# Attention's 64-token halves on the two halves of the partitions, merged TensorE visits, and an earlier start of the first MLP

## The chip, the cores and the metric

One NeuronCore of a Trainium2 chip. The metric is the device time of one execution in microseconds, median of the runs given. Engine names in the profile: PE is TensorE, PEld its weight loads, DVE VectorE, ACT ScalarE, POOL GpSimd, SP SyncE (it issues the DMAs).

## The reference

4 sequences of 768 tokens, 8 heads of 32 columns. A gated linear attention runs over them in chunks with a carried 16 x 32 state per head; its output, [3072, 256], passes a gated MLP (RMS norm, 1536 hidden) and a second MLP (2048 hidden).

```python
y_intra = einsum('bhij,bhjd->bhid', CB * L, xc)            # L: decays inside the chunk, causal
y_inter = einsum('bhin,bhnd->bhid', Cc, state) * decay_to_i
state = decay_full * state + sum_j(Bc_j xc_j decay_from_j)
xn = x / sqrt(mean(x*x) + 1e-6) * rms_g                      # x: the attention's output
x = (silu(xn @ w_gate) * (xn @ w_val)) @ w_out
out = ((x @ w_in) * clip(x @ w_in + 3, 0, 6) / 6) @ w_out2
```

The weights arrive as 64-bit floats.

## The kernel before, in words

**Tiling.** The attention is cut into 24 chunks of 128 tokens (4 sequences, 6 positions); each chunk is two halves of 64 tokens. Four chunks, one of each sequence, make a block of 512 tokens. The first MLP (stage A) runs over 6 blocks x 12 steps of 128 hidden columns, the second (stage B) over 6 blocks x 16 steps. Each matrix product is done as three fp32r products of high and low parts (`mm3`, L640 to L643): a group of six matmuls of 512 columns. A step of stage A (`step`, L647) has three groups: two `hidden` (gate and value, into `hps`) and one `result` (into `acc`); a step of stage B has one of each two kinds. Between them ScalarE applies Silu or Relu (`gate`, L668), VectorE multiplies (`prod`, L676), ScalarE makes the high part (`hi`, L684) and GpSimd or VectorE the low part (`lo`, L688, recorded at L242).

**A chunk** (`attention`, L319) loads one packed tensor (`cb`, 1152 columns, in which the two heads of a pair are padded with zeros), the decays `L` and the prefix products `P`. For the first four chunks the decays are spread over the partitions by TensorE (`spread_a`, L354, tile `aps`), later ones come by DMA from a copy in DRAM (`azero`). VectorE runs the product scan (L367). TensorE is visited three times: `score` (L389) with `grow` (L407), `inner` (L450), and `mean` (L480, the sum of squares of each token). Each of these fp32 matmuls leaves two records in the trace.

**The norm of a block** (`norm`, L502): on [128, 4] scalars VectorE does the inverse root (for block 0 ScalarE's Sqrt and a reciprocal, later a guess by integer arithmetic and three Newton rounds, with `y` in PSUM), TensorE broadcasts the result (`back`, L531, tile `rps`), VectorE scales x (L537), and `split` (L560) makes high and low parts.

**PSUM.** Two banks for `acc` and three pairs of banks (`w`), which the chunks (two pairs each) and the MLP's steps (one pair each) take in turns.

**What sets the order.** `Plan` (L33) is a list scheduler: every operation is entered with engine costs in ns, with what it reads and writes, and with a boost. It goes through simulated time, takes on each engine the operation with the longest tail plus boost, and emits all in that order, so each engine's queue is fixed. Buffers taken in turns also fix the order of their first writers (L64). Attention of the next block carries a boost of 6000, that of the first block 15000 (L28, L29); weights (`weights`, L579: load, four conversions, high and low part) carry none. `AT` (L26) says behind which step of a block the next block's chunks and norm are entered. While TensorE has nothing in the plan's first part, `fill` (L156) puts in idle matmuls (`idle`, L303). The loop over all this is at L748 to L776.

## Time and profile before

| | us |
|---|---|
| median of 3 runs | 679.15 |
| lowest and highest run | 677.57, 680.35 |
| span of the profiled execution | 677.3 |

The profile is that of one execution, of which no other time than its span is listed. TensorE is busy 97% of the span, VectorE and ScalarE 44%, GpSimd 42%. Matmuls overlap, so a record of 0.39 us stands for about 0.23 us of TensorE's time when others follow; lengths are therefore read from start to start. In a row of stretches the first number is the length, then each engine's busy us with its count.

### The profile page before, as it was taken

To read this page: it belongs to the slowest core of one execution; us is meant where nothing else is said; L and a number is where in the kernel's file an instruction comes from. 1 tells how busy PE (TensorE), PEld (TensorE's weight loads), DVE (VectorE), ACT (ScalarE), POOL (GpSimd) and SP (SyncE) were. 2 spreads that over 40 slices of the span, in tenths; PEclk is the share of its full clock that TensorE was granted. 3 is DMA by queue.
4 is the path that set the end of the run, shared out by engine and by line. 5 is a ranking of instruction groups with operands and counts; after the bars stand their busy time and mean duration, and the time that the engine had idled before them with its cause. 6 is when DMAs were issued, how large, how long until landed. Compare 5 with 4: busy or idle time off the path is not lost.

```text
span 677.3 us, 10507 instructions
## 1 busy us (share of the span) xinstructions
PE 657.6 (97%) x4188; PEld 529.0 (78%) x4188; DVE 301.0 (44%) x507; ACT 298.2 (44%) x494; POOL 282.7 (42%) x239
## 2 busy tenths in 40 slices
PE   8978999999999999999999999999999999999997
PEld 7856777778778778877867777888888888888886
DVE  4799853352234334332578773232322322332222
ACT  1576632322333223313366654445454545445543
POOL 3354453333433332432232435455454545545443
PEclk9888999999999999999999999999999999999999
DMA  5995203210221123030023420000000000000000
GB/s 196 318 320 188 95 1 95 70 55 20 91 67 44 56 65 100 1 118 1 0 94 125 142 76 0 1 0 32 1 0 32 0 32 0 1 32 0 32 0 32
DMA packets 24465, 42.92 MB, mean 63 GB/s; under 512 B 2112, under 2 KB 15712, under 8 KB 24416
## 3 DMA queue, kind: packets, MB, share of 16 engines
q1 hardware_dynamic: 24416, 42.25, 19.2%
q8 instruction: 33, 0.54, 0.3%
q14 instruction: 16, 0.13, 0.1%
HBM read 38.90 MB, written 3.34 MB: 62 GB/s over the span
## 4 chain that ended last, share of the span: by engine, by line
PE 80%; DVE 10%; ACT 3%; issue 3%; DMA 2%; POOL 1%; SPq 0%; POOLq 0%; ACTq 0%; DVEq 0%
PE hps L643 41%; PE acc L643 30%; DVE cv L608 2%; PE sps L394 2%; PE sps L463 2%; DMA L<-azero 1%; DVE cv L603 1%; DVE p L679 1%; ACT p L671 1%; PE sps L457 1%; PE sps L482 1%; DVE yT L608 1%; POOL gl L242 1%; PE sps L412 1%; PE aps L359 1%
## 5 line engine op out<-in xcount | busy, mean ns | idle before, releaser
L242 POOL TENSOR_TENSOR gl<-p,gh 128x512 fp32r<-128x512 f32 x160 | 214.3, 1341 | 239.8 <-ACT gh L686 233.1
L686 ACT CAST gh<-p 128x512 fp32r<-128x512 f32 x168 | 104.5, 622 | 94.7 <-PE acc L643 92.0
L681 DVE SCALAR_TENSOR_TENSOR p<-p,hps 128x512 f32<-128x512 f32 x96 | 65.9, 687 | 170.1 <-ACT p L673 170.1
L643 PE MATMUL hps<-xh,w1h 128*128 128x512 f32 x288 | 96.3, 416 | 7.9 <-ACT p L671 4.8
L673 ACT ACTIVATE p<-hps,half 128x512 f32<-128x512 f32 x96 | 66.3, 691 | 83.8 <-POOL gl L242 82.9
L679 DVE TENSOR_TENSOR p<-p,hps 128x512 f32<-128x512 f32 x72 | 49.3, 685 | 97.7 <-PE hps L643 75.8
L643 PE MATMUL hps<-xh,w1l 128*128 128x512 f32 x288 | 90.2, 395 | 0.0
L643 PE MATMUL hps<-xl,w1h 128*128 128x512 f32 x288 | 89.9, 393 | 0.0
L643 PE MATMUL acc<-gh,w2h 128*128 128x512 f32 x192 | 74.7, 389 | 0.0
L643 PE MATMUL acc<-gh,w2l 128*128 128x512 f32 x192 | 74.7, 389 | 0.0
L643 PE MATMUL acc<-gl,w2h 128*128 128x512 f32 x192 | 74.7, 389 | 0.0
L671 ACT ACTIVATE p<-hps 128x512 f32<-128x512 f32 x72 | 43.0, 597 | 64.6 <-POOL gl L242 33.2
L643 PEld LDWEIGHTS hps<-xh,w1h 128*128 128x128 f32 x288 | 50.0, 190 | 24.6 <-ACT p L671 8.9
L643 PEld LDWEIGHTS hps<-xh,w1l 128*128 128x128 f32 x288 | 54.6, 189 | 12.4
L643 PEld LDWEIGHTS hps<-xl,w1h 128*128 128x128 f32 x288 | 54.6, 190 | 12.3
L643 PE MATMUL hps<-xh,w2h 128*128 128x512 f32 x192 | 59.6, 391 | 1.5 <-DVE p L679 0.8
L643 PE MATMUL hps<-xl,w2h 128*128 128x512 f32 x192 | 59.2, 389 | 0.0
L643 PE MATMUL hps<-xh,w2l 128*128 128x512 f32 x192 | 59.1, 389 | 0.0
L643 PE MATMUL acc<-gh,w1h 128*128 128x512 f32 x144 | 59.0, 410 | 0.0
L643 PE MATMUL acc<-gl,w1h 128*128 128x512 f32 x144 | 56.3, 391 | 0.0
L643 PE MATMUL acc<-gh,w1l 128*128 128x512 f32 x144 | 56.2, 390 | 0.0
L242 POOL TENSOR_TENSOR bh<-cb,L 128x256 f32<-128x256 f32 x24 | 17.1, 713 | 76.4 <-PE sps L412 48.3
(94 smaller groups left out, 814.3 us busy)
## 6 DMA issues: line engine op xcount, KB each, us to landing
cb<-comb SPq DMA_DIRECT2D x20, 576.0 KB, 8.1
raw<-w SPq DMA_DIRECT2D x16, 512.0 KB, 3.4
L<-azero SPq DMA_DIRECT2D x40, 128.0 KB, 3.3
yT<-w SPq DMA_DIRECT2D x6, 768.0 KB, 9.2
rawx<-w SPq DMA_DIRECT2D x6, 768.0 KB, 9.7
out<-yT SPq DMA_DIRECT2D x12, 256.0 KB, 2.0
P<-pref SPq DMA_DIRECT2D x24, 64.0 KB
cb<-comb SPq DMA_DIRECT2D x4, 320.0 KB, 4.0
```

What stands on the lines that cost most here:

```text
L242: eng[e].tensor_tensor(out=out, in0=a, in1=b, op=op)
L359: pe.matmul(out=ps[64 * q:64 * q + 64, p * CH:(p + 1) * CH], rhs=az[:, q], lhsT=eye[:96, c:c + 1].to_broadcast([96, SC]), start=True, stop ...
L394: pe.matmul(out=bank2(ws[p // 2], "sps")[:, p % 2, c * SC:(c + 1) * SC], lhsT=cb[r, BN + c * 128:BN + (c + 1) * 128], rhs=cb[r, CT + c * S ...
L412: pe.matmul(out=v()[32 * p:32 * p + 32, 1, 384 + 64 * c:448 + 64 * c], lhsT=b[:, h], rhs=cb[:, 64 * (4 * c + p):64 * (4 * c + p) + 64], st ...
L463: pe.matmul(out=o[p][c], lhsT=cb[:, q:q + 64], rhs=SM[:, p, SC * c:SC * c + SC], start=False, stop=True, skip_group_check=True)
L608: dve.scalar_tensor_tensor(out=u, in0=T[kr].bitcast(I32)[:, :, 1], scalar=-0x80000000, in1=u, op0=ALU.bitwise_and, op1=ALU.bitwise_or)
L643: pe.matmul(out=o, lhsT=a, rhs=c, start=first and i == 0, stop=last and i == len(seq) - 1)
L671: act.activation(out=p[:, :n], in_=T["w", hid][:, 0, :n], func=AF.Silu)
L673: act.activation(out=p[:, :n], in_=T["w", hid][:, 0, :n], func=AF.Relu, scale=1.0 / 6.0, bias=half)
L679: dve.tensor_tensor(out=p, in0=p, in1=h, op=ALU.mult)
L681: dve.scalar_tensor_tensor(out=p, in0=p, scalar=1.0, in1=h, op0=ALU.min, op1=ALU.mult)
L686: act.copy(out=t[:, :n], in_=T["p", i][:, :n])
```

## The change

- The two halves of a chunk lie on partitions 0 to 63 and 64 to 127. `cb` shrinks to 896 columns: C is padded now, x and B are not. Score has 8 matmuls of 32 rows, 64 weight columns and 128 moving columns (before: 128 and 64); grow 8 of 64 rows (before 128); inner 16 of 64 rows and 32 weight columns and 8 of 32 rows as before. VectorE masks the grown state (`mask`).
- A visit of TensorE does `score` and `grow` of chunk k and `inner` of chunk k - 1, with a drain inside `inner`. A block has four visits (the first block one more).
- The norm works on [128, 512]: high and low parts of the squares, four matmuls with a matrix of ones, then all further steps at full width in SBUF; for block 0 it is done chunk by chunk at 128 columns.
- The first four chunks load `L` from the input and clip it; `spread_a` goes.
- PSUM: in the start two pools of four banks for chunks; then two `acc` banks, two single `h` banks for the MLP, four for chunks; from step 9 of the last block but one on four `hb` banks in place of these.
- Weight tiles 0 and 1 carry boosts of 12000 and 10000. ScalarE reads the Silu table behind the last root of block 0.
- The idle matmuls only begin when the start's PSUM pool closes.

```diff
-AT = {0: 0, 2: 1, 4: 2, 6: 3, 8: 4}
+W0 = 12000
+AT = [1, 3, 5, 7]
+AT_NORM = 8
+NCB = 3
...
-            fn, ns, t, cold, until = self.fill
+            fn, ns, after, cold, until = self.fill
+            t = 1 + next(s for s, i, _, _ in out if i == after)
+            cold += t
...
-    ps_acc = ctx.enter_context(tc.tile_pool(name="ps_acc", bufs=1, space=PSUM))
-    ps_w = ctx.enter_context(tc.tile_pool(name="ps_w", bufs=3, space=PSUM))
+    ps_at = att.enter_context(tc.tile_pool(name="ps_at", bufs=1, space=PSUM, side="right"))
+    ps_0 = early.enter_context(tc.tile_pool(name="ps_0", bufs=1, space=PSUM))
...
+        def ld_L(e):
...
+            src = azero if k >= B else ablk
+            for c in range(2):
+                nc.sync.dma_start(out=flat(t[64 * c:64 * c + 64]),
+                                  in_=src[c, k].partition_broadcast(SC))
...
+        def clip(e):
+            t = T["L", k]
+            eng[e].tensor_scalar(out=t, in0=t, scalar1=1e-6, scalar2=1.0, op0=ALU.max, op1=ALU.min)
+            eng[e].memset(t[:, :, 0:1], 0.0)
...
+    def score(k):
+        cb, o = T["cb", k], part(k, 0, 128)
+        for c in range(2):
+            for p in range(4):
+                r = slice(32 * p, 32 * p + 32)
+                pe.matmul(out=o[64 * c:64 * c + 64, p],
+                          lhsT=cb[r, BN + c * SC:BN + (c + 1) * SC],
+                          rhs=cb[r, CP + c * CH:CP + (c + 1) * CH],
+                          start=True, stop=True, skip_group_check=True)
+
+
+    def grow(k):
+        cb, b, o = T["cb", k], flat(T["bh", k]), part(k, 192, 64)
+        for p in range(4):
+            for c in range(1 if k >= NK - B else 2):
+                r = slice(64 * c, 64 * c + 64)
+                pe.matmul(out=o[32 * p:32 * p + 32, c], lhsT=b[r, 32 * p:32 * p + 32],
+                          rhs=cb[r, XX + 64 * p:XX + 64 * p + 64],
+                          start=False, stop=True, skip_group_check=True)
...
+    def inner(k, apart=False):
+        cb, SM, y = T["cb", k], T["SM", k], part(k, 128, 64)
+
+        def intra(t):
+            for g in range(4):
+                for c in range(2):
+                    h, r = 4 * t + g, slice(64 * c, 64 * c + 64)
+                    pe.matmul(out=y[32 * g:32 * g + 32, 2 * t + c], rhs=SM[r, h],
+                              lhsT=cb[r, XX + D * h:XX + D * h + D],
+                              start=False, stop=True, skip_group_check=True)
+
+        intra(0)
+        intra(1)
+        if apart:
+            pe.drain()
+        for c in range(1 if k < B else 0, 2):
+            for p in range(4):
+                r, q = slice(32 * p, 32 * p + 32), p % 2 * 64
+                pe.matmul(out=y[q:q + 64, p // 2 * 2 + c], lhsT=before(k, c)[r, :],
...
+    def mean(o, j, cols):
+        n = 0
+        for s in ("sqh", "sql"):
             for t in range(2):
...
+                pe.matmul(out=o, lhsT=ones, rhs=T[s, j][:, t, cols], start=n == 0, stop=n == 3,
+                          skip_group_check=True)
...
+        P.op({"PE": 908}, total, r=[("sq", j, i, u) for i in range(B) for u in range(2)],
+             w=[("h", hn)], boost=bst)
+        P.op({"ACT": a1(512)}, shift, r=[("h", hn)], w=[v], boost=bst)
+        P.op({"DVE": d2(512) + d1(512)}, guess, r=[v], w=[y, z], boost=bst)
+        for _ in range(3):
+            newton(j, cols, (v, y, z), None, None, bst, 512)
...
+    P.op({"ACT": 1400}, lambda e: act.activation(out=spare, in_=half, func=AF.Silu),
+         r=[("rn", 0, k, 2) for k in range(B)], w=[("table", 0)], boost=BOOST0)
...
-                lambda f: yflat[:, 4608 + f % 2 * 768:5376 + f % 2 * 768], w1h, w1l)
+                lambda f: yflat[:, 4608 + f % 2 * 768:5376 + f % 2 * 768], w1h, w1l,
+                bst=(W0 - 2000 * f if f < 2 else 0))
+
+    def visit(k):
+        new, old = k < NK, k > B
...
+        def go(e):
+            if new:
+                score(k)
+                grow(k)
+            if old:
+                inner(k - 1, new)
+
+        P.op({"PE": 1500 if new and old else 950}, go, r=r, w=w, boost=BOOST)
+        if old:
+            finish_chunk(k - 1)
+        if new:
+            middle(k)
...
+            if j == 0 and f == 0:
+                visit(B)
+            if f in AT:
+                visit((j + 1) * B + 1 + AT.index(f))
+            if f == AT_NORM:
                 xb.append(nxt(nx))
                 norm(j + 1, xb[j + 1])
+                if j == NB - 2:
+                    P.op({"HOST": 0}, open2, r=xkeys[xb[-1]], w=[("open", 2), ("open", 0)])
+                    late.append(1)
```

## Rows read from the trace of the kernel before

**Rows 1.** Busy times of the page, part 1: us (share of the span) xinstructions.

```profile
PE 657.6 (97%) x4188; PEld 529.0 (78%) x4188; DVE 301.0 (44%) x507; ACT 298.2 (44%) x494; POOL 282.7 (42%) x239
```

**Rows 2.** Stretches, L643 alone: A:B length, PE busy (xcount), PEld, PEclk, DMA share, GB/s.

```profile
31.20:84.00 52.80, 35.27 (x127) 24.04 (x127) 0.94 0.68 211
...
164.50:209.10 44.60, 35.39 (x139) 24.84 (x138) 1.00 0.27 84
...
421.80:673.66 251.86, 251.86 (x1110) 208.29 (x1110) 1.00 0.03 11
```

**Rows 3.** Timeline about the first group: start, us, engine, line, op, [idle before <-releaser].

```profile
31.23 0.71 PE L643 MATMUL hps<-xh,w1h 128*128 128x512 f32 x2
...
34.23 0.83 ACT L246 CAST w1h<-yT 128x768 fp32r<-128x768 f32 x1 [2.47 <-DVE yT L608]
35.08 1.28 ACT L671 ACT_TABLE_LOAD   x1
...
36.37 0.60 ACT L671 ACTIVATE p<-hps 128x512 f32<-128x512 f32 x1
...
37.02 0.74 PE L643 MATMUL hps<-xh,w1h 128*128 128x512 f32 x2 [3.18 <-ACT p L671]
```

**Rows 4.** TensorE's timeline, one chunk of the fourth block's attention, then the norm's broadcast.

```profile
164.57 0.67 PE L394 MATMUL sps<-cb 32*128 32x64 f32 x16
165.18 0.43 PE L412 MATMUL sps<-cb,bh 128*32 128x64 f32 x16
165.54 0.73 PE L643 MATMUL hps<-xh,w1h 128*128 128x512 f32 x2
...
167.12 0.46 PE L457 MATMUL sps<-ch,V 32*64 32x64 f32 x16
167.51 0.69 PE L463 MATMUL sps<-SM,cb 128*64 128x64 f32 x16
168.13 0.50 PE L643 MATMUL acc<-gh,w1h 128*128 128x512 f32 x1
...
169.62 0.50 PE L482 MATMUL sps<-ones,sq 128*128 128x1 f32 x4
169.99 0.49 PE L643 MATMUL acc<-gh,w1h 128*128 128x512 f32 x1
...
171.47 0.62 PE L643 MATMUL hps<-xh,w1h 128*128 128x512 f32 x2
...
208.32 1.05 PE L533 MATMUL rps<-eye,y 128*128 128x128 f32 x8
209.13 0.71 PE L643 MATMUL hps<-xh,w1h 128*128 128x512 f32 x2
```

**Rows 5.** TensorE's timeline in the start: the broadcast of decays for one chunk.

```profile
14.93 1.09 PE L359 MATMUL aps<-az,eye 96*64 96x128 f32 x16
```

**Rows 6.** Stretches, all engines: length, PE, PEld, DVE, ACT, POOL busy, PEclk, DMA, GB/s.

```profile
0.00:31.20 31.20, 28.08 (x371) 24.76 (x372) 18.18 (x43) 10.79 (x20) 10.50 (x22) 0.95 0.77 249
31.20:84.00 52.80, 46.23 (x410) 35.10 (x408) 48.79 (x71) 35.53 (x52) 25.89 (x18) 0.94 0.68 211
164.50:209.10 44.60, 44.29 (x418) 34.74 (x418) 17.12 (x44) 12.82 (x25) 15.34 (x15) 1.00 0.27 84
```

**Rows 7.** VectorE: two groups (busy us, mean ns), and L242's forms (ns min/median/max).

```profile
L679 DVE TENSOR_TENSOR p<-p,hps 128x512 f32<-128x512 f32 x72 | 49.3, 685 | 97.7 <-PE hps L643 75.8 <-ACT p L671 21.5
...
L526 DVE TENSOR_TENSOR z<-z,rps 128x4 f32<-128x4 f32 x16 | 2.5, 158 | 0.6
...
L242 DVE TENSOR_TENSOR xl<-xT,xh x7: 693/1655/1771, 29.6 to 334.2; 128x512 fp32r<-128x512 f32 x7
```

**Rows 8.** DMA issues of the page, part 6: queue, xcount, KB each, us to landing.

```profile
L<-azero SPq DMA_DIRECT2D x40, 128.0 KB, 3.3
```

**Rows 9.** Stretches, matmuls into hps (first row) and into acc (second): PE busy (xcount).

```profile
31.20:209.10 177.90, 102.30 (x390) 0.98 0.34 105
...
31.20:209.10 177.90, 42.88 (x162) 0.98 0.34 105
```

More of the change, by code (lines that the diff above doesn't have):

```diff
@@ new lines, in scale, with norm_chunk, shift @@
+    def scale(e, j, t, cols):
+        x = T["xT", j][:, t, cols]
+        dve.scalar_tensor_tensor(out=x, in0=x, scalar=gs[:, t:t + 1], in1=rn(j)[1][:, cols],
+                                 op0=ALU.mult, op1=ALU.mult)
+    def norm_chunk(k, b):
+        s, bst, cols = place(k)[0], BOOST0, slice(k * CH, k * CH + CH)
+        m = lambda: part(k, 0, 128)[:, 0]
+        v, y, z = (("rn", 0, k, n) for n in range(3))
+        def shift(e):
+            dve.tensor_scalar(out=rn(0)[0][:, cols], in0=m(), scalar1=1.0 / DM, scalar2=1e-6,
@@ L553, in norm @@
-        for t in range(2):
-            P.op({"DVE": d1(512) + 60}, lambda e, t=t: scale(e, t),
-                 r=[("xT", j, i) for i in range(B)] + [("w", wn, 1), ("cs", 0)],
-                 w=[("xT", j, -1, t)], boost=bst)
+            dve.reciprocal(out=rn(0)[1][:, cols], in_=rn(0)[2][:, cols])
+        P.op({"PE": 600}, lambda e: mean(m(), 0, cols),
+             r=[("sq", 0, k, 0), ("sq", 0, k, 1)], w=[s + (0,)], boost=bst)
+        P.op({"DVE": d1(128)}, shift, r=[s + (0,)], w=[v], boost=bst)
@@ L643, in mm3, with hid @@
             pe.matmul(out=o, lhsT=a, rhs=c, start=first and i == 0, stop=last and i == len(seq) - 1)
-    nstep, prev = [0], []
+    nstep, prev, late = [0], [], []
+    def hid(n):
+        if ("h",) + n not in T:
+            T[("h",) + n] = mlp[2 if n[0] == "hb" else 1].tile([128, 512], F32, tag=n[0], name="hps")
+        return T[("h",) + n]
     def step(ph, b, f, n, acc):
```

507 lines of the change are left out of this document (250 added, 257 removed).

## The prediction

> **What bounds the kernel now.** I read the busy times first: TensorE (PE) is busy 97% of 677.3 us, every other engine 44% or less [rows 1]. Then I cut the span into stretches and counted only the matmuls of the two MLP stages, L643 [rows 2]. From 421.8 to 673.66 us there is nothing but these: 251.86 us for 1110, so 0.227 us each, or 1.36 us for a group of six. All 2448 cost 2448 x 0.227 = 555 us; no part of the change touches that. What can move is the other 122 us: 31.2 us before the first group [rows 3], about 4 us after the last, and what is pushed between groups of the first MLP stage. For the stretch 164.5 to 209.1 (next block's attention) that is 44.6 - 139 x 0.227 = 13.1 us; three more such stretches, one a block, look the same, and the first (31.2 to 84.0) has 52.8 - 127 x 0.227 = 24.0 us, as TensorE also waits there.
>
> One chunk shows where the 13.1 us go [rows 4]. Score and grow take 0.97 us (164.57 to 165.54), inner 1.01 (167.12 to 168.13), mean 0.37 (169.62 to 169.99), and the group behind each is slow: 1.58, 1.49 and 1.48 us in place of 1.36, 0.47 together. That is 2.82 a chunk, 11.3 for four; the broadcast of the norm adds 0.81 (208.32 to 209.13): 12.1, with 1.0 in smaller gaps. PE is thus the bound, and a visit costs its own time and its return.
>
> **The change, part by part; all sums on the profiled execution, span 677.3 us.** No other time of that execution is given; the span lies 1.85 us under the median of the runs, 679.15, and I add that to the forecast.
>
> *Merged visits.* Thirteen interruptions a block (4 x 3 and the broadcast) become five: four visits and one sum of squares. No row has the new shapes, so each gets bounds. A record is one of the two that each of these fp32 matmuls leaves. Score: 16 records, 32 rows by 64 weight columns, 128 moving columns. The nearest in array shape is L457, 16 in 0.39 us [rows 4]; the nearest in moving columns is L359, 16 in 1.09 us [rows 5]. It lies nearer the first, as it spreads over row and column groups alike: 0.50. Grow: still 16 records of 32 columns: 0.36 as L412. The intra-chunk product: 32 records with 32 weight columns: 0.72 at the rate of L412 (0.36 for 16), 1.24 at that of L463 (0.62 for 16); I take 0.72 for the same width. The carried-state product keeps its shape: 0.39. The drain between them: none to see at the changes of shape in [rows 4], where the return to the full array costs 0.22, so 0 to 0.2; I take 0.05. A visit is about 2.0 us (bounds 1.6 and 2.9), with one slow return 2.2. The sum of squares becomes four groupable matmuls of 512 columns: 4 x 0.227 = 0.91, 1.0 with its return. A block: 4 x 2.2 + 1.0 = 9.8 against 12.1, and of the 1.0 in small gaps 0.4 goes with the fewer visits: -2.7. Five blocks: -13.5 us (one extra half visit is in the noise). With the bounds of a visit, -21.5 and +4.5. A merged visit also has to wait for both chunks' inputs, and the groups queued behind it with it; before, PE was idle 0.3 us of 44.6 in such a stretch [rows 6], so I price that at nothing; should scan or decay come late, the whole MLP would wait behind the visit, and that is in the upper bound.
>
> *Fewer PSUM banks.* The MLP step gets two single banks in place of three pairs. A chunk in flight holds two of the three pairs today, and PE is still busy in the stretch of [rows 4]. The second half of a step needs the product (0.69 us, L679 [rows 7]) of the step before, with 2.7 us of PE work between: nothing.
>
> *The start.* Per chunk the norm becomes [128,128] work on VectorE (DVE): seven operations and a mask. Between 0.158 us at 4 columns and 0.685 at 512 [rows 7], 128 columns is about 0.29: 4 x 8 x 0.29 = 9.3 us, and clipping up to 4 x 0.69 = 2.7. DVE did 18.2 us before 31.2 [rows 6], part of it the old norm and work for later blocks. The first L now comes by a transfer, 3.3 us from issue to landing [rows 8], so some 3.5 us pass before DVE's chain begins. If none of the 18.2 dropped out, the first group would come at 3.5 + 18.2 + 12.0 = 33.7 us, packed without a gap; if half of it did, at 24.6. I take about 29.5, the middle. The eight loads of L are eight more issues on SyncE's queue, each ahead of later chunks' loads, and chunk 3's loads still wait for chunk 0's buffers; that is in the waits between the ends, as is the clock, since the filler matmuls now come only right before the first group. So -1.7 us; ends -6.6 and +2.5.
>
> *Two tiles early, Silu table early.* In 31.2 to 84.0, 24.0 - 13.1 = 10.9 us are neither groups nor visits: 52.80 - 46.23 = 6.6 idle [rows 6], the rest the clock: 0.94 in the mean, so about an eighth of the stretch was granted 1.2 in place of 2.4 GHz. The longest wait, 3.18 us, ends with the first gate [rows 3]: it stood in ScalarE's queue behind a weight cast that waited 2.47 us for DVE and behind a table load of 1.28 us. Both leave this place, with perhaps 1 us of clock: -4.2. What is late next is DVE: 48.79 of 52.80 us busy there [rows 6], and the next norm adds 9 x (0.69 - 0.16) = 4.8 us of Newton, less one tile's conversion; I give back 0.7. So -3.5; ends -7 and +3. The table load: it is the row's 1.28 us, the gate starting 0.01 us behind it. The Trainium skill (ScalarE: Activation LUTs, What ACT_TABLE_LOAD costs) puts a switch at some 2.66 us, of which about half is a drain; the trace shows no such drain, and by the page the term would be larger by 1.4 us.
>
> *The later norms.* The sum is 0.91 us; shift, two guesses, nine Newton operations, two scalings and a split in two follow one another on 512 columns, 16 x 0.69 = 11.0 [rows 7]; some 2 for handing over and 2 for the MLP's products between them: 16 us. Cover: at 209.1 the hidden matmuls stand at 390/12 = 32.5 steps, the result matmuls at 162/6 = 27 [rows 9]. So seven hidden groups of the block are left and about as many result groups whose inputs are ready: 14 x 1.36 = 19 us. Covered by 3 us, mostly: +1 (0 to +10). In the last block but one, steps 9 to 11 are planned behind that norm and its four fresh banks hold two steps; the work that is left on PE is some ten groups, 13.6 us of 16: +2.5 with a slower clock behind it (0 to +8).
>
> Sum: -13.5 - 1.7 - 3.5 + 1 + 2.5 = -15.2: span 662.1, forecast **664 us**.
>
> **Rivals.**
> (a) *Visits are much cheaper*: the eight pieces of the array overlap well, 1.5 us with the return, as the planner's new entry has it (its old ones, 1,100, 1,000 and 550, stand near [rows 4]). Then 4 x 0.7 x 5 = 14 us more is gained: 650. For: L412 and L457 run at 23 to 25 ns a record. Against: twice the moving columns in score, 48 records in inner.
> (b) *The early work doesn't come early*: DVE is full in the start, tiles 0 and 1 are done no sooner, the first group stays at 31 us and its stall too: 5 us worse, 669.
> (c) *Visits gain nothing*: 80 records at the dear rates, 2.9 us and a return: net +4.5 for the visits, 682: no change.
> (d) *Slower: the norm becomes the bound.* In the old Newton one operand was in PSUM; now both are in SBUF, as in xl<-xT,xh, which takes 0.69 us at best and 1.66 in the median: I take it that GpSimd, which subtracts the other half at the same time, is what slows it; p<-p,hps, with one operand in PSUM, stays at 0.69 [rows 7]. Each of the eleven operations that meets it costs 0.97 us more. If all do, the chain is 16 + 10.7 = 26.7 us: 7.7 beyond its cover in four blocks and 13 in the last, 44 us: 704. It decides from six of eleven on (a chain of some 21.7 us), where the waits eat all that is gained. Against: GpSimd is busy 15.3 of 44.6 us [rows 6], so fewer than half should meet it. The Trainium skill (SBUF — State Buffer, SBUF: two separate sides) says that the two engines lock one another out of a shared port pair for a whole instruction if DVE reads two SBUF tensors; the 0.69 and 1.66 agree.
>
> **Chances.** Forecast 0.46 (656 to 671), (a) 0.22, (b) 0.12, (c) 0.10, (d) 0.10. The range reaches over (a) and (b) and to the edge of (c): 647 to 678. About 0.5% is what a measurement of this kernel can tell from no change: faster (below 675.8) 0.80, within 0.10, slower 0.10.
>
> **What would show it.** Right: five interruptions a block, some 10 us in place of 13.1; a visit of 2 us; the first group before 31 us and no 3 us wait for the first gate; Newton mostly at 0.7 us. Wrong: visits near 3 us; PE waiting at each block's start for xh or xl; the first stage slowed by products that are late on DVE.

## The result and the profile after

The changed kernel takes 689.62 us in the median of four runs (689.42 to 690.27), the kernel before 678.84 beside it (677.57 to 680.35): a ratio of 1.0145, 95% interval 1.0119 to 1.0171. It is slower by about 10 us, where the prediction said 664 and faster. The profiled execution has a span of 687.4 us (its own time 689.42); before it was 677.3, so 10.1 us are to be found.

The busy times of the page, part 1, answer to [rows 1]:

```profile
PE 630.7 (92%) x4366; PEld 503.6 (73%) x4366; DVE 372.3 (54%) x527; ACT 304.5 (44%) x515; POOL 309.5 (45%) x263
```

TensorE does 27 us less than before, and the span is 10 us longer: time went from work to waiting. VectorE (DVE) has 71 us more. To see where, I cut both spans at two events: the first group of the MLP, and the moment at which a block's accumulators begin to be read. First the kernel after, all engines (A:B length, then PE, PEld, DVE, ACT, POOL busy, PEclk, DMA share, GB/s): start, first block of stage A, blocks 1 to 4. They answer to [rows 6].

```profile
0.00:40.28 40.28, 17.83 (x330) 13.93 (x331) 28.36 (x65) 12.99 (x26) 19.93 (x28) 1.00 0.81 262
40.28:138.80 98.52, 82.93 (x728) 61.98 (x728) 84.88 (x99) 48.10 (x78) 45.90 (x36) 0.93 0.29 91
138.80:386.00 247.20, 234.85 (x2023) 185.53 (x2016) 142.34 (x201) 91.88 (x176) 99.98 (x90) 0.98 0.16 54
```

The same view of the kernel before, first block and blocks 1 to 4 (its start of 31.20 us is in [rows 6]):

```profile
31.20:128.10 96.90, 90.15 (x763) 69.33 (x762) 68.21 (x103) 48.99 (x78) 44.49 (x35) 0.96 0.44 137
128.10:376.10 248.00, 243.81 (x1761) 192.11 (x1759) 111.67 (x219) 86.00 (x158) 82.92 (x72) 1.00 0.19 62
```

So the start is 9.1 us longer, the first block 1.6, blocks 1 to 4 are 0.8 shorter, and the rest (301.4 against 301.2) is the same: 10.1 in all. Nearly the whole loss is in the start; and in blocks 1 to 4, which hold four of the five sets of cheaper visits, nothing is left of the gain. To see why, one more cut: the MLP's matmuls alone in blocks 1 to 4, before (L643) and after (L706), and after in stage B (answering to [rows 2]).

```profile
128.10:376.10 248.00, 214.14 (x873) 159.22 (x871) 1.00 0.19 62
```

```profile
138.80:386.00 247.20, 211.38 (x879) 166.69 (x880) 0.98 0.16 54
...
440.00:683.70 243.70, 243.70 (x1076) 201.52 (x1074) 1.00 0.03 11
```

A matmul costs 0.227 us at full rate, as before. That splits the four blocks into four parts (each rounded by itself): the matmuls at full rate, what they take beyond it (slow returns behind a visit, half clock), other work on TensorE (the visits), and idle time. "Products first" is an experiment below, put beside them here.

| blocks 1 to 4, us | before | after | products first |
|---|---|---|---|
| matmuls at 0.227 us | 198.2 (873) | 199.5 (879) | 199.5 (879) |
| beyond that rate | 16.0 | 11.9 | 6.3 |
| visits and norm on TensorE | 29.7 | 23.5 | 23.4 |
| idle | 4.2 | 12.4 | 5.5 |
| sum | 248.0 | 247.2 | 234.7 |

The visits are cheaper by what the change promised, and idle time has taken it. One visit in the first block, and the sum of squares (TensorE's timeline: start, us, line, operation, records; answering to [rows 4]):

```profile
63.36 0.47 PE L385 MATMUL sps<-cb 32*64 32x128 f32 x16
63.76 0.34 PE L396 MATMUL sps<-cb,bh 64*32 64x64 f32 x16
63.90 0.59 PE L411 MATMUL sps<-SM,cb 64*32 64x64 f32 x32
64.59 0.46 PE L422 MATMUL sps<-ch,V 32*64 32x64 f32 x16
64.98 0.73 PE L706 MATMUL hps<-xh,w1h 128*128 128x512 f32 x2
...
95.37 0.62 PE L508 MATMUL rps<-sqh,ones 128*128 128x512 f32 x2
...
96.29 0.39 PE L706 MATMUL acc<-gh,w1h 128*128 128x512 f32 x1
```

From start to start a visit is 64.98 - 63.36 = 1.62 us (forecast 2.0) and the sum of squares 0.92 (forecast 0.91). Now the idle time: who ends it. TensorE's waits in blocks 1 to 4 (in total, times, longest), the kernel after:

```profile
PE hps L706 <- DVE p L747: 8.7, 4, 2.3
PE hps L706 <- ACT p L739: 2.2, 2, 1.6
```

Before:

```profile
PE hps L643 <- DVE p L679: 2.0, 4, 0.9
```

The longer waits are for the product p on VectorE, once a block. This is block 1; p needs the gate's half and a second hidden group, whose last two matmuls start at 172.07: what VectorE and GpSimd (POOL) did ahead of the late product, and TensorE's wait (timelines: start, us, idle before in brackets).

```profile
165.90 1.82 POOL L235 TENSOR_TENSOR gl<-p,gh 128x512 fp32r<-128x512 f32 x1 [3.71 <-ACT gh L754]
...
165.89 0.69 DVE L235 TENSOR_TENSOR z<-z,y 128x512 f32<-128x512 f32 x1
166.61 1.66 DVE L528 SCALAR_TENSOR_TENSOR y<-z,y 128x512 f32<-128x512 f32 x1
...
169.03 1.72 DVE L235 TENSOR_TENSOR z<-z,y 128x512 f32<-128x512 f32 x1
...
171.28 1.04 DVE L528 SCALAR_TENSOR_TENSOR y<-z,y 128x512 f32<-128x512 f32 x1
172.35 1.42 DVE L537 SCALAR_TENSOR_TENSOR xT<-xT,gs,y 128x512 f32<-128x512 f32 x2
173.68 0.68 DVE L442 TENSOR_TENSOR SM<-sps,L 128x512 f32<-128x512 f32 x1
174.45 1.22 DVE L235 TENSOR_TENSOR xl<-xT,xh 128x512 fp32r<-128x512 f32 x1
175.59 0.68 DVE L747 TENSOR_TENSOR p<-p,hps 128x512 f32<-128x512 f32 x1
...
172.07 0.62 PE L706 MATMUL hps<-xl,w1h 128*128 128x512 f32 x2
...
176.32 0.73 PE L706 MATMUL hps<-xh,w1h 128*128 128x512 f32 x2 [2.28 <-DVE p L747]
```

Between 171.28 and 175.59 VectorE works through the norm's last instructions, a decay and a split, without a gap. The product's inputs are there at 172.69 (172.07 + 0.62), so it stands in the queue for 2.9 us; both single banks stay full, and TensorE, whose order is fixed too, waits. The wait costs twice: the clock falls. The MLP's matmuls in the stretch right behind it (the third last number is PEclk, the granted clock as a share of the full 2.4 GHz):

```profile
176.32:181.24 4.92, 4.92 (x15) 3.91 (x15) 0.65 0.13 44
```

15 matmuls in 4.92 us in place of 15 x 0.227 = 3.4: 1.5 us more. Blocks 2 and 3 show the same (waits of 2.28 and 2.35 us, a mean of 0.65 of the full clock behind them).

The start, answering to [rows 3] (timelines of several engines):

```profile
6.19 1.91 POOL L343 TENSOR_SCALAR L<-L 128x512 f32<-128x512 f32 x1 [3.22 <-DMA L<-ablk]
...
8.31 1.23 DVE L361 TENSOR_TENSOR_SCAN L<-L,eye 128x512 f32<-128x512 f32 x1 [4.08 <-POOL L L344]
...
9.62 0.41 POOL L235 TENSOR_TENSOR bh<-cb,L 128x128 f32<-128x128 f32 x1 [1.34 <-DVE L L361]
10.12 1.92 POOL L343 TENSOR_SCALAR L<-L 128x512 f32<-128x512 f32 x1
...
16.52 2.71 POOL L343 TENSOR_SCALAR L<-L 128x512 f32<-128x512 f32 x1
...
19.43 1.73 DVE L361 TENSOR_TENSOR_SCAN L<-L,eye 128x512 f32<-128x512 f32 x1 [1.46 <-POOL L L344]
...
35.99 1.28 ACT L820 ACT_TABLE_LOAD   x1
...
40.28 0.73 PE L706 MATMUL hps<-xh,w1h 128*128 128x512 f32 x2 [1.78 <-ACT xh L239]
...
44.28 0.74 PE L706 MATMUL hps<-xh,w1h 128*128 128x512 f32 x2 [0.99 <-ACT p L739]
```

The planner put all four clips on GpSimd, at a price of 900 ns; one takes 1.91. The first three stand in one chain: clip, scan on VectorE, bh on GpSimd (which needs the scan), and only then the next clip, some 3.9 us a chunk; the fourth clip takes 2.71. The fourth scan starts at 19.43, in the kernel before at 16.14. From there to the first group, after and then before (all engines, as above):

```profile
19.43:40.28 20.85, 12.66 (x170) 10.50 (x170) 19.76 (x47) 9.78 (x19) 7.57 (x9) 1.00 0.96 338
```

```profile
16.14:31.20 15.06, 14.18 (x201) 13.09 (x198) 10.63 (x25) 8.54 (x16) 4.93 (x6) 0.89 0.98 312
```

So 3.3 of the 9.1 us are lost up to the fourth scan and 5.8 behind it, where VectorE is busy 19.8 of 20.9 us, before 10.6 of 15.1. The early table load is there, and the first gate's wait fell from 3.18 to 0.99 us, but 9 us later.

### The profile page after: what moved, and what is told of

The parts are those of the page before. It is cut to its first block, busy times and chain, and to the rows that moved or that the text cites. A ratio compares the mean times of both kernels' runs of the same rounds, so it can differ in the third digit from the quotient of the medians.

```text
span 687.4 us, 10943 instructions
## 1 busy us (share of the span) xinstructions
PE 630.7 (92%) x4366; PEld 503.6 (73%) x4366; DVE 372.3 (54%) x527; ACT 304.5 (44%) x515; POOL 309.5 (45%) x263
## 4 chain that ended last, share of the span: by engine, by line
PE 68%; DVE 16%; ACT 4%; issue 3%; DMA 1%; DVEq 0%; ACTq 0%; SPq 0%
PE hps L706 36%; PE acc L706 27%; DVE p L747 2%; DVE y L528 2%; DVE cv L665 2%; DVE cv L660 1%; DVE xT L537 1%; DMA raw<-w 1%; PE sps L422 1%; DVE z L235 1%; DVE yT L665 1%; DVE z L520 1%; PE sps L385 1%; PE sps L411 1%; ACT cv L652 1%
## 5 line engine op out<-in xcount | busy, mean ns | idle before, releaser
L235 POOL TENSOR_TENSOR gl<-p,gh 128x512 fp32r<-128x512 f32 x158 | 210.6, 1333 | 253.9 <-ACT gh L754 251.2
L706 PE MATMUL hps<-xh,w1h 128*128 128x512 f32 x288 | 95.4, 413 | 22.6 <-DVE p L747 17.5
L706 PE MATMUL hps<-xh,w1l 128*128 128x512 f32 x288 | 93.3, 407 | 2.2 <-POOL w1l L235 2.2
L706 PE MATMUL hps<-xl,w1h 128*128 128x512 f32 x288 | 92.3, 403 | 0.0
L706 PEld LDWEIGHTS hps<-xh,w1h 128*128 128x128 f32 x288 | 53.3, 194 | 40.5 <-DVE p L747 22.3
L706 PE MATMUL acc<-gh,w2h 128*128 128x512 f32 x192 | 74.7, 389 | 0.0
L706 PE MATMUL acc<-gh,w2l 128*128 128x512 f32 x192 | 74.7, 389 | 0.0
L706 PE MATMUL acc<-gl,w2h 128*128 128x512 f32 x192 | 74.7, 389 | 0.0
L706 PEld LDWEIGHTS hps<-xh,w1l 128*128 128x128 f32 x288 | 56.2, 196 | 15.3 <-POOL w1l L235 3.1
L706 PEld LDWEIGHTS hps<-xl,w1h 128*128 128x128 f32 x288 | 56.5, 196 | 12.6
L706 PE MATMUL hps<-xh,w2h 128*128 128x512 f32 x192 | 59.6, 392 | 2.5 <-ACT p L739 1.9
L706 PE MATMUL hps<-xl,w2h 128*128 128x512 f32 x192 | 59.2, 389 | 0.0
L706 PE MATMUL hps<-xh,w2l 128*128 128x512 f32 x192 | 59.1, 389 | 0.0
L706 PE MATMUL acc<-gh,w1h 128*128 128x512 f32 x144 | 57.6, 400 | 0.0
L706 PE MATMUL acc<-gh,w1l 128*128 128x512 f32 x144 | 56.7, 394 | 0.0
L706 PE MATMUL acc<-gl,w1h 128*128 128x512 f32 x144 | 56.6, 393 | 0.0
L706 PEld LDWEIGHTS hps<-xh,w2h 128*128 128x128 f32 x192 | 35.7, 188 | 11.3 <-ACT p L739 2.7
```

Of the source, the lines that this page charges most:

```text
L235: eng[e].tensor_tensor(out=out, in0=a, in1=b, op=op)
L706: pe.matmul(out=o, lhsT=a, rhs=c, start=first and i == 0, stop=last and i == len(seq) - 1)
```

## The experiments

Eighteen runs. Ratios are to the kernel before, run beside them; its medians there are 678.84 to 681.14 us, so a difference of up to 2 us between two rows says nothing by itself. The planner writes one order for the whole kernel, so an edit of one price or rank moves work everywhere; the cuts of each profile are therefore given in us: first group of the MLP, first block, blocks 1 to 4, rest.

| run | first group | first block | blocks 1 to 4 | rest | median | ratio (95%) |
|---|---|---|---|---|---|---|
| before | 31.2 | 96.9 | 248.0 | 301.2 | 678.84 | |
| after | 40.3 | 98.5 | 247.2 | 301.4 | 689.62 | 1.0145 (1.0119 to 1.0171) |
| e1 clips on VectorE | 37.7 | 95.4 | 245.4 | 300.8 | 681.58 | 1.0011 (0.9990 to 1.0032) |
| e2 late tiles | 41.6 | 98.5 | 245.4 | 300.9 | 689.73 | 1.0125 (1.0091 to 1.0158) |
| e3 no early table | 40.5 | 97.9 | 244.9 | 301.4 | 687.58 | 1.0108 (1.0081 to 1.0134) |
| e4 one Newton round | 40.3 | 93.9 | 230.6 | 300.5 | 667.16 | 0.9797 (0.9772 to 0.9823) |
| e5 products first | 40.0 | 94.8 | 234.7 | 300.9 | 673.26 | 0.9892 (0.9860 to 0.9924) |
| e6 unmerged | 40.1 | 100.1 | 257.6 | 301.8 | 701.88 | 1.0307 (1.0276 to 1.0337) |
| e7 before, two banks | 44.3 | 87.4 | 247.8 | 303.6 | 684.60 | 1.0062 (1.0040 to 1.0083) |
| e8 squares on ScalarE | 40.3 | 95.9 | 239.7 | 301.4 | 678.92 | 0.9974 (0.9957 to 0.9992) |
| e9 = e8 + e1 | 36.5 | 93.4 | 240.5 | 300.9 | 672.01 | 0.9875 (0.9841 to 0.9909) |
| e10 = e9 + e5 | 37.6 | 94.7 | 237.9 | 300.9 | 670.46 | 0.9861 (0.9835 to 0.9886) |
| e11 = e10, measured prices | 39.0 | 76.7 | 252.6 | 301.9 | 672.27 | 0.9879 (0.9856 to 0.9902) |
| e12 = e10, late tiles | 37.7 | 93.1 | 237.9 | 300.9 | 671.60 | 0.9867 (0.9840 to 0.9893) |
| e13 = e16, gates first | 36.2 | 98.7 | 235.4 | 300.8 | 672.58 | 0.9895 (0.9868 to 0.9922) |
| e14 = e13 + e8 | 36.9 | 97.2 | 238.8 | 301.4 | 674.76 | 0.9923 (0.9894 to 0.9953) |
| e15 before, ranks | 31.4 | 101.7 | 252.7 | 301.2 | 689.29 | 1.0145 (1.0111 to 1.0179) |
| e16 = e5 + e1 | 36.2 | 96.4 | 234.5 | 301.5 | 670.80 | 0.9872 (0.9841 to 0.9903) |
| e17 narrow norm | 40.5 | 101.6 | 256.5 | 300.0 | 704.75 | 1.0348 (1.0313 to 1.0382) |
| e18 = e17 + e1 | 36.6 | 95.9 | 259.0 | 298.9 | 692.41 | 1.0177 (1.0136 to 1.0218) |

**Clips on VectorE (e1).**

```diff
-            P.op({"DVE": d2(512) + 70, "POOL": 900}, clip, r=[("L", k)], w=[("L", k)], boost=bst)
+            P.op({"DVE": d2(512) + 70}, clip, r=[("L", k)], w=[("L", k)], boost=bst)
```

> The four clips of the first attention run on VectorE instead of GpSimd; nothing else is edited. Theory 1 (the series clip, scan, bh, clip on GpSimd at about 3.9 us a chunk sets the start): with clips of about 0.3 us the four scans end near 15 us instead of 21.2 and the first group of the MLP starts at 33 to 36 us instead of 40.28; the time falls by 4 to 7 us, to 683 to 686. Theory 2 (the loads and VectorE's own work of 28.4 us set the start, and the clips only fill waits): the first group stays at 39 us or later and the time within 1.5 us of 689.6.

681.58 us, 8.0 less. The time fell by more than theory 1 says, and a clip is 0.43 us (its line in this run: ns min/median/max, first and last start):

```profile
L343 DVE TENSOR_SCALAR L<-L x4: 426/427/427, 6.0 to 15.5; 128x512 f32<-128x512 f32 x4
```

But the first group starts at 37.7, only 2.6 us earlier, and not at 33 to 36. The fourth scan does come early, at 16.05, as in the kernel before; from there to the first group:

```profile
16.05:37.70 21.65, 12.90 (x178) 10.29 (x179) 18.19 (x46) 10.55 (x21) 6.20 (x9) 1.00 0.91 310
```

That way is 6.6 us longer than before, with VectorE busy 18.2 us of it for 10.6. The other 5.5 us of the gain come from the first block (3.1), blocks 1 to 4 (1.8) and the rest (0.6), where the edit touches nothing: the planner's other order. So the clips on GpSimd explain 2.6 of the start's 9.1 us here, and 3.8 or 3.9 in the pairs e5 and e16, e8 and e9, e17 and e18; the rest lies behind the scans, and no run takes it away.

**Late tiles (e2).** The first two weight tiles have no rank over the first attention.

```diff
-                bst=(W0 - 2000 * f if f < 2 else 0))
+                bst=0)
```

> The first two weight tiles get no priority over the first attention any more; the early Silu activation stays. Theory 1 (their four VectorE conversions of about 0.9 us stand ahead of the last reciprocals and Newton steps, so they delay the last xh by about what they save afterwards): the last xh comes 2 to 4 us earlier, the first group waits about 2 to 4 us for its weights behind it, and the time is within 2 us of 689.6. Theory 2 (early conversion is worth what I forecast): 2 to 4 us slower, 692 to 694. Theory 3 (early conversion is itself the loss at the start): 3 us or more faster, under 686.6.

689.73 us, the time of the changed kernel. The first group comes at 41.6, 1.3 us later than with early tiles and not earlier; the first block is as long. The early tiles are worth nothing that shows.

**No early table (e3).** The Silu activation of L820 is left out; the gates read the table.

> The kernel after the change without its early Silu activation, so ScalarE reads the table with the first gate again. If the read counts, the first gate comes 1.3 us later behind the first group and the time rises by 1 to 3 us; if the gate waits for weights and products anyway, within 1 us of 689.6.

687.58 us, 2 us faster, which neither reading says; the two intervals overlap, and the difference lies in blocks 1 to 4, far from the read. The early read is worth nothing that can be measured.

**One Newton round (e4).**

```diff
-        for _ in range(3):
+        for _ in range(1):
             newton(j, cols, (v, y, z), None, None, bst, 512)
```

> The norms of blocks 1 to 5 make one Newton round instead of three: six full-width VectorE instructions of 0.7 to 1.7 us a block are left out. Theory 1 (the products stand behind the norm on VectorE, and so TensorE waits): the stalls of 2.3 to 3.0 us near 115, 176, 238 and 300 us and the half-clock stretches behind them go, 3 to 5 us for each, and the time falls by 10 to 18 us, to 672 to 680. Theory 2 (two single banks leave no slack whatever VectorE carries): the stalls stay at over 1.5 us each and the time falls by under 4 us.

667.16 us, 22.5 less and more than either theory said. Blocks 1 to 4 fall from 247.2 to 230.6, TensorE idles 2.2 of them, and its wait for products there is 0.5 us in place of 8.7:

```profile
134.20:364.80 230.60, 228.38 (x2021) 182.06 (x2014) 121.28 (x176) 93.39 (x177) 96.58 (x89) 1.00 0.18 59
```

With the norm's instructions out of the way, the visits' gain comes through in full, with the same two banks.

**Products first (e5).**

```diff
-        P.op({"DVE": d1(n)}, prod, r=[hs[-1], ("p", i)], w=[("p", i)])
+        P.op({"DVE": d1(n)}, prod, r=[hs[-1], ("p", i)], w=[("p", i)], boost=20000)
```

> The products of the MLP go ahead of everything else on VectorE in the planner's order (a boost of 20000); nothing is left out. Theory 1 (it is the order: a product stands behind norm or attention instructions while both single banks are full): TensorE's wait for products, 17.5 us in the kernel after the change, falls under 7 us, and the time falls by 8 to 15 us, to 675 to 682. Theory 2 (it is the amount: the planner's prices for VectorE are too low, so it sees no need to choose and the instructions come late whatever the rank): the wait stays over 13 us and the time within 3 us of 689.6, or the norm is late in its place and TensorE waits for xh and xl at the start of a block.

673.26 us, 16.4 less; nothing is left out, VectorE is as busy in blocks 1 to 4 (141.9 us against 142.3), only the order is another. Theory 1, by more than it said. TensorE is busy 229.3 of 234.7 us at a granted clock of 1.00:

```profile
134.80:369.50 234.70, 229.25 (x2023) 182.32 (x2016) 141.88 (x207) 91.84 (x176) 92.67 (x85) 1.00 0.18 57
```

Its wait for products there (8.7 us before this edit; over the whole of stage A 6.6 in place of 17.5):

```profile
PE hps L706 <- DVE p L747: 1.8, 1, 1.8
```

In the first block VectorE is nearly full in this order too (81.7 of 94.8 us): TensorE still idles 16 us there, most for products (4.5 us), for weights whose low part GpSimd makes (4.1) and for masks (3.9); only the clock is better, 0.98 for 0.93.

**Unmerged (e6).** Score, grow and inner are three operations of the planner again, with a drain behind inner.

```diff
...
-        P.op({"PE": 1500 if new and old else 950}, go, r=r, w=w, boost=BOOST)
+        if new:
+            r, w = front_keys(k)
+            P.op({"PE": 700}, lambda e: score(k), r=r[:1], w=w[:1], boost=BOOST)
+            P.op({"PE": 500}, lambda e: grow(k), r=r + w[:1], w=w[1:], boost=BOOST)
+        if old:
+            r, w = back_keys(k - 1)
+            P.op({"PE": 1000}, lambda e: (inner(k - 1, True), pe.drain()), r=r, w=w, boost=BOOST)
```

> Scores, state growth and the inner part of a chunk are again three operations of the planner (with a drain behind the inner part), so TensorE is interrupted up to three times for a chunk instead of once. Theory 1 (merging saves interruptions): about 1 us more for a chunk, 15 to 25 us slower over 20 chunks if all three come apart, 5 to 12 us if the planner leaves two together. Theory 2 (the gain of the visits is the smaller matmuls alone, merging adds nothing): within 2 us of 689.6.

701.88 us, 12.3 more. Merging is worth something of itself (one more drain included). Blocks 1 to 4:

```profile
140.20:397.80 257.60, 237.48 (x2048) 180.11 (x2048) 144.75 (x214) 90.04 (x172) 85.49 (x85) 1.00 0.16 52
```

The visits' own work is about that of the merged kernel (237.48 - 213.06 for the MLP's matmuls = 24.4 us); their time beyond 0.227 us each is 213.06 - 880 x 0.227 = 13.3, and 20.1 us are idle. Against the merged kernel these blocks are 10.4 us longer, 7.7 of it idle: TensorE now also waits for xT (3.7 us in three waits) and at the carried-state product (2.2 us in eleven, with no releaser in the profile). For the slow returns products first is the fairer neighbour, at the same granted clock of 1.00: 13.3 against 6.3 us.

**The kernel before with two banks (e7).** A hidden group of stage A gets one of two single banks, chunks share two pairs.

```diff
-    ps_w = ctx.enter_context(tc.tile_pool(name="ps_w", bufs=3, space=PSUM))
+    ps_w = ctx.enter_context(tc.tile_pool(name="ps_w", bufs=2, space=PSUM))
+    ps_h = ctx.enter_context(tc.tile_pool(name="ps_h", bufs=2, space=PSUM))
...
-        hid, nv = nxt(nw), 2 if A else 1
+        nv = 2 if A else 1
+        hs = [("h", nxt(nh)) if A or i % 2 else ("w", nxt(nw), 0) for v in range(nv)]
...
```

> The kernel before with the PSUM of the change: a hidden group of stage A gets one of two single banks, a chunk of attention one of two pairs (instead of three pairs for both); norm, attention and order of the edits are those of before. Theory 1 (two single banks cost nothing by themselves as long as VectorE has room, 24 of 62 us busy in a block): within 3 us of before. Theory 2 (the lost third pair is itself the cause of the waits for products): TensorE's wait for products in stage A rises from 3.5 us to over 12 us, and the time by 8 to 20 us.

684.60 us, ratio 1.0062: 3 to 6 us over before, between the two theories. But blocks 1 to 4 take 247.8 us against 248.0:

```profile
131.60:379.40 247.80, 245.62 (x1890) 194.94 (x1889) 106.77 (x223) 83.94 (x152) 86.92 (x78) 1.00 0.20 63
```

In these blocks the bank question is decided for the old norm: with it on VectorE, two single banks cost nothing, and TensorE's wait for products in stage A did not rise (0.4 us, before 3.5). With the new norm's long queue no run gives more than two banks, so what a third pair would have covered stays open. The difference is start and first block together (131.6 against 128.1) and the rest with another set of buffers in stage B (303.6 against 301.2).

**Squares on ScalarE (e8), and with the clips (e9).** In the full-width rounds the first two instructions become z = y * y on ScalarE and z = -0.5 * z * v on VectorE.

```diff
+        if n == 512:
...
+                act.activation(out=z, in_=y, func=AF.Square)
...
+                dve.scalar_tensor_tensor(out=z, in0=z, scalar=-0.5, in1=u, op0=ALU.mult, op1=ALU.mult)
...
+            P.op({"ACT": a1(n)}, sq, r=[y], w=[z], boost=bst)
+            P.op({"DVE": d1(n)}, bv, r=[z, v], w=[z], boost=bst)
```

> In the full-width Newton rounds of blocks 1 to 5 the square of y is taken by ScalarE (busy 20 of 62 us in a block) instead of a product with two SBUF inputs on VectorE; three instructions a block move, nothing is left out. By what one Newton round less gave (22.4 us for thirty instructions of VectorE, 0.75 us for each), theory 1 (VectorE's load in the blocks of stage A) expects 15 fewer to give 7 to 13 us, 677 to 683. Theory 2 (the norm's own length as a chain is what counts, not VectorE's load): the chain gets no shorter, three more hand-overs between the engines come in, and the time stays within 3 us of 689.6 or gets worse.

> The squares on ScalarE and the clips of the first attention on VectorE together. If the two are independent (start and stage A), their gains add: 8.0 us for the clips and 7 to 13 us for the squares, 668 to 675, faster than the kernel before. If both draw on the same slack of VectorE in the first block, the sum is 4 us or more short of that.

678.92 and 672.01 us: 10.7 and 17.6 less. Both in the range of VectorE's load; the chain's length (theory 2 of e8) did not rule. The clips add 6.9 of their 8.0 us in the time, though again only 3.8 of the sum lies in the start.

**All three, and variants (e10, e11, e12).** e11 prices VectorE as measured (65 + 1.21 ns an element, 65 + 2.6 for a scan, 940 for a reciprocal); e12 drops the early tiles' rank.

> Products first, squares on ScalarE and clips on VectorE together, all of the computation kept. Alone they gave 16.4, 10.7 and 8.0 us. Theory 1 (order and load are two halves of one cause, the start another): order and squares share their gain, the clips add theirs, 660 to 666. Theory 2 (all three independent): the sum of 35 us, 653 to 657. Theory 3 (once products go first, VectorE is no longer the bound and nothing else counts): the time of products first, 670 to 674.

> As the run with all three, but the planner is given VectorE's durations as this trace shows them (0.69 us for a full-width instruction of two inputs, 1.4 us for a scan, 0.94 us for a reciprocal). If wrong prices are what is left of the waits for VectorE in the first block and at the start, 3 to 6 us faster than with all three; if the priority of the products has made the prices unimportant, within 2 us of it.

> As the run with all three, but without the priority of the first two weight tiles over the first attention. In the kernel after the change that priority was worth nothing (689.7 to 689.6 us), while GpSimd's clips set the start. With the clips on VectorE, theory 1 (VectorE is now the bound of the start, and four conversions of 0.9 us stand in it): the norm ends 2 to 4 us earlier, but the first group then waits for weights, within 2 us of the run with all three. Theory 2 (the early tiles are worth what I forecast once nothing else sets the start): 2 to 4 us slower than it.

670.46, 672.27 and 671.60 us, with intervals that overlap. Theory 3 of e10 has the number, the time of products first, but not the reason: the clips still count, 3.8 us at the start in e16. Beside the rank exact prices buy nothing, nor do early tiles; exact prices without the rank were not run. (e11's planner moves attention from the first block into the next, so its two cuts shift against each other.) In e10 it is now gates that TensorE waits for most (all of stage A):

```profile
PE hps L719 <- ACT p L752: 7.3, 7, 2.1
PE hps L719 <- DVE p L760: 4.2, 7, 1.8
```

The squares rank ahead of the gates on ScalarE (with products first alone the wait for gates is 4.5 us). Is it the same fault, one engine further? The next runs ask.

**Ranks on both engines (e16, e13, e14), and in the kernel before (e15).** e16 is products first and clips; e13 has gates first too; e14 is e13 with the squares; e15 ranks gates and products first in the kernel before.

> Products first and clips on VectorE, the Newton rounds as they were. If the squares on ScalarE are what spoils the run with all three (gates late behind them), this run is faster than it: 665 to 668, the two gains of 16 and 8 us added on 689.6. If the squares help even here, it is slower than 670.5.

> As the run with products first and clips on VectorE, and the gates first on ScalarE too. If late gates cost time in the first block, where ScalarE converts weights (4.5 us of waits for gates with products first), 2 to 5 us faster than without; if ScalarE has slack enough, within 1.5 us of it.

> The run with all three, with the gates first as well. If late gates behind the squares are what held it at 670.5, the 7.3 us of waits for gates go and the time falls to 662 to 667. If it stays within 2 us of 670.5, something else holds it, such as the visits' chunks coming later because their VectorE work now ranks behind.

> The kernel before with gates and products first in its own schedule. If the change itself (full-width norm on VectorE, two single banks) made the rank matter, the kernel before gains little: within 4 us of 680.6, since TensorE waits there only 8 us for gates and products in all. If the rank was a fault of both, it gains 8 us or more.

670.80, 672.58, 674.76 and 689.29 us, and none is what I expected. e16 ties with e10: the gains of 16 and 8 us do not add (18.8). Gates first are 1.8 (intervals overlap) and 4.3 us slower than without, so late gates were not what held e10. And the rank makes the kernel before neither better nor the same, but 9.8 us slower (689.29 against 679.50 beside it): there it pushes back other instructions that TensorE waits for: the carried state in the first block (6.5 us in two waits, without the rank 0.5), and the old norm's small ones at its broadcast (blocks 1 to 4; 1.2 us without the rank):

```profile
PE rps L533 <- DVE y L527: 4.6, 3, 2.3
```

By these runs a rank is no gain of itself: it pays where what it overtakes has cover, as the full-width norm has, and costs where TensorE waits for what was overtaken.

**The old norm in the changed kernel (e17, e18).** Sums of squares into four columns, Newton on 128x4, four matmuls that spread the result; e18 with the clips.

```diff
+            for q in range(B):
+                for n, (s, u) in enumerate((s, u) for s in ("sqh", "sql") for u in range(2)):
+                    pe.matmul(out=t[:, q:q + 1], start=n == 0, stop=n == 3, skip_group_check=True,
+                              lhsT=T[s, j][:, u, q * CH:q * CH + CH].bitcast(F32),
+                              rhs=ones[:, 0:1].bitcast(F32))
...
-            newton(j, cols, (v, y, z), None, None, bst, 512)
+            newton(j, slice(0, B), (v, y, z), None, None, bst, B)
+        P.op({"PE": 350 * B}, back, r=[y], w=[("h", hm)], boost=bst)
...
```

> The norm of blocks 1 to 5 as in the kernel before: sums of squares into four columns with the tokens on the partitions (sixteen matmuls of one column), Newton rounds on 128x4, and four matmuls with an identity that spread the result; all of the computation is kept and the planner's ranks are those of the change. Theory 1 (VectorE's full-width norm is the step that cost the gain): eleven instructions of 0.43 to 1.7 us a block go and about 3 us of TensorE come back, so at least what one Newton round less gave, less 5 blocks by 2 to 3 us: 668 to 680. Theory 2 (two single banks and the order of VectorE cost as much whatever the norm is, or the norm's second hold on one of the two banks costs more): 684 or more.

> The same with the clips of the first attention on VectorE. If start and stage A lose separately, 2.6 us (the start alone) to 8 us (what the clips gave alone) faster than the narrow norm alone; if the clips' 8 us came mostly from another order in the first block, as the combinations suggest, it is within 3 us of it.

704.75 and 692.41 us: theory 2 of e17; and e18 gains 12.3 us by the clips, more than either reading said (the profiled executions differ by 8.2 only: 3.9 at the start, 5.7 in the first block and 1.1 in the rest, less 2.5 in blocks 1 to 4). The sums of squares go from 0.92 us on TensorE to 3.5 (164.13 to 167.62), the spread adds 0.9, and a product is still late (TensorE and VectorE, block 1):

```profile
164.13 0.50 PE L595 MATMUL rps<-ones,sqh 128*128 128x1 f32 x4
...
167.62 0.48 PE L728 MATMUL acc<-gh,w1h 128*128 128x512 f32 x1
...
174.51 1.69 DVE L236 TENSOR_TENSOR xl<-xT,xh 128x512 fp32r<-128x512 f32 x1
176.12 0.43 DVE L461 SCALAR_TENSOR_TENSOR V<-V,P,um 128x64 f32<-128x64 f32 x1
176.48 2.31 DVE L365 TENSOR_TENSOR_SCAN L<-L,eye 128x512 f32<-128x512 f32 x1
178.71 0.66 DVE L769 TENSOR_TENSOR p<-p,hps 128x512 f32<-128x512 f32 x1
...
179.42 0.90 PE L728 MATMUL hps<-xh,w1h 128*128 128x512 f32 x2 [2.00 <-DVE p L769]
```

VectorE is busy 121.9 of 256.5 us here, 20 less than after the change, and the product still stands behind a split, a state and a scan, 2.0 us late. So the share of busy time isn't what decides; what stands ahead of the product in the queue is. As a cure this failed; it does not tell what the full-width norm alone costs, since it changed TensorE's work too and takes a second hold on one of the two banks.

## Why the prediction was wrong

The measured span is 25.3 us over the forecast one (687.4 against 662.1). By the cuts 10.8 of it lie at the start, 7.8 in the first block (forecast -3.5 - 2.7, measured +1.6), 6.5 in blocks 1 to 4 (forecast -10.8 + 1 + 2.5, measured -0.8) and 0.2 in the rest. Two steps failed: the fewer banks, priced at nothing, and the start, priced with almost no waits of VectorE.

**Merged visits: right, and sized too small.** I took 2.2 us with the return, 2.7 us gained a block, 10.8 in four. A visit measures 1.62 from start to start, and its return is some 0.15 slower. My bounds for it, 1.6 and 2.9, are not what its pieces add up to (1.9 and 3.3); score took 0.40 (taken: 0.50), grow 0.14 (0.36), the intra-chunk product 0.69 (0.72) and the state's 0.39. In the table of blocks 1 to 4, visits and returns together fall from 29.7 + 16.0 to 23.4 + 6.3 once no product is late: 15.9 us. Five interruptions a block were right, and the sum of squares was right to 0.01 us. Rival (a) was nearer than my choice. Three fifths of the gain (9.7 us) are slow returns that do not happen, the pieces of the visits only 6.2; e6 fits, with 13.3 us beyond the full rate.

**Fewer PSUM banks: the step that failed.** I wrote that "The second half of a step needs the product (0.69 us, L679 [rows 7]) of the step before, with 2.7 us of PE work between: nothing." The instruction's own 0.69 us was compared with the slack, not the queue in front of it. At 171.28 to 175.59 VectorE had five other instructions of the norm and the visit to do first, 4.3 us, of which the product stood ready for 2.9. By the code's ranks the four of the norm (y, two of xT, xl) are above the product; the decay SM is below it, and goes first because it is ready first in the planner's time. Two banks with the old norm cost nothing in those blocks (e7); the same load in another order costs little (e5); the long queue on two banks costs 12.5 us in blocks 1 to 4 (247.2 - 234.7): 6.9 of it idle (12.35 - 5.45) and 5.6 beyond the full rate (11.9 - 6.3), 4.5 of which are the lower clock behind the three waits (1.5 each). That the order does it is shown (e5); that more banks would not have covered it is not. Neither view alone shows this: it takes the step's slack, the product's place in the planner's order and the length of what stands ahead of it. The first and the last can be read from rows of before and their 128x512 durations, the second from the code; I put only the first in the sum.

**The later norms: right where I looked.** The chain I put at 16 us runs from 160.23 (sum of squares) to 175.67 (end of xl), 15.4, and TensorE never waits for xh or xl at the start of a block: the cover was there. I charged the norm as a chain that could be late, and it cost as a load that made something else late. Rival (d) had the price right, an instruction with two SBUF inputs taking 0.69 or about 1.7 us when GpSimd is at work (166.61 beside gl at 165.90, 169.03 beside one at 168.94); but three or four of eleven meet it, not six, and the place was wrong. The Trainium skill (SBUF — State Buffer, SBUF: two separate sides) says that VectorE with two SBUF inputs and GpSimd lock one another out of a shared port pair for a whole instruction; these rows agree. Of my signs for "wrong", the last one came true: "the first stage slowed by products that are late on DVE". I had it as a sign and not as a term.

**The last block but one** (+2.5): about right. TensorE waits 0.59, 1.82 and 1.57 us in 322.6 to 386.0 (at 357.91, 369.86 and 381.26) for gates and products, 4.0 in all, where its cut of the kernel before has 2.0. Products first leaves these three as they are; they are 4.0 of the 5.5 us idle in e5.

**The start: a step that failed, by 10.8 us and with the wrong sign.** I forecast -1.7 (ends -6.6 and +2.5) and got +9.1. My 29.5 us were 3.5 of waiting and 26.0 of VectorE's work without a gap; measured are 11.9 and 28.4. So 8.4 of the 10.8 us are waits for which my sum had no term beyond the 3.5, though rows of before hold them: VectorE idles 13.0 of its 31.2 us there (31.2 - 18.2 [rows 6]). After the change 10.8 of the 11.9 lie before the fourth scan, 8.6 in the kernel before; behind it the work comes without gaps, but too late to fill them. The clips lengthen these waits: the planner could put a clip on either engine, at 900 ns on GpSimd; no row showed that clip, and I did not bound it there. It takes 1.91. That explains 2.6 us (e1). The work is 2.4 us more than I took: I priced every 128x128 instruction at 0.29 us, and the four reciprocals are 0.94 each, 2.6 us more. That VectorE's work behind the fourth scan (19.8 us for 10.6) sets the first group is read from the trace; no run takes it away.

**Early tiles and table** (-3.5): the gate's long wait went as forecast (3.18 to 0.99), and nothing came of it: the first block is 1.6 us longer although its visits and other TensorE work fall by 7.4 us ((90.15 - 73.30) - (82.93 - 73.46), with 73.30 and 73.46 the MLP's matmuls there). Idle rises from 6.8 to 15.6 us: products (8.6 us) and masks (3.0) from VectorE, busy 53.8 of the first 55.1 us, weights from GpSimd (2.2) and a gate from ScalarE (1.0). I had noted it as 48.8 of 52.8 us busy "next" and gave back 0.7. Without the early tiles (e2) or the early table (e3) the time is the same or lower.

**What stays open.** One Newton round and products first each bring out nearly all of the visits' gain in blocks 1 to 4 (230.6 and 234.7). Combinations stop at about 670 us. Each edit re-plans start and first block, where VectorE is nearly full; that this is the reason is not shown, and a cure for these two was not found. The best versions here, e10 and e16, beat both kernels: 1.0 to 1.65% faster than before by their intervals, with the whole computation kept.

## What to carry to other kernels

A buffer is long enough only against the consumer's queue, not against the consumer's own duration: before you call fewer buffers free, list what can stand ahead of the consumer on its in-order engine, by its place in the schedule, and set that sum against the slack. Work moved off the bounding engine lands on another; charge it first to whatever that engine releases, and only then as a chain of its own. And when a scheduler chooses between engines by a price list, check the price of every new choice against a row, since a wrong one moves the work silently.

## What the runs showed of the hardware

A max-min clip of 128x512 fp32 takes 1.91 us on GpSimd and 0.43 on VectorE, 4.5 times as long. The Trainium skill (Trainium Architecture — The Big Picture, The five engines, in one table) has GpSimd at half of VectorE's speed for streaming elementwise work. For a product or difference of two tensors the rows are near it (1.27 us on GpSimd at 168.94, 0.69 on VectorE at 165.89); for this clip they are not, and the measurement decides. A reciprocal of 128x128 takes 0.94 us where other VectorE instructions of that size take 0.28. A TensorE wait of 2.3 us is followed by about 5 us at a mean granted clock of 0.65, between the two levels of 1.2 and 2.4 GHz, which costs another 1.5 us: a stall on that engine is dearer than it looks in the waits. A scan of 128x512 is 1.23 us at 8.31 and 2.31 in e17 at 176.48, where GpSimd's gl starts within 0.05 us of it.
